# An SSM convolution with a gated feed-forward block, forward and backward: weight transposes through DRAM in pieces, stores on another queue, and gate tiles in rotating roles

## The chip, the core and the metric

The kernel runs on one core of a Trainium2 chip. A core has engines with queues of their own that work in parallel: TensorE (PE: matmuls; its weight loads are shown as PEld), VectorE (DVE), ScalarE (ACT), GpSimd (POOL) and SyncE (SP). SP, ACT and POOL also issue transfers (DMAs) between on-chip memory (SBUF) and DRAM; all of them are carried by the same 16 DMA engines. Matmul results go to PSUM, whose banks are shared out among the stages. Each queue is executed in order: an instruction that waits holds up everything behind it.

The metric is the time of one execution on the device in microseconds (us). Lower is better.

## What is computed

The reference is a forward pass and its vector-Jacobian product. With L = 2048, D = 576, F = 4608 and N = 128:

```python
x  = A_u                                   # [1, 2048, 576]
xn = layernorm(x)
# A: diagonal state-space model as a long convolution
K  = einsum("dn,dnl,dn->dl", C, exp(dt*A*l), dt*B).real
s  = irfft(rfft(xn, 2L) * rfft(K, 2L))[:L] + xn * Dskip
# B: gated feed-forward block
gate, up = xn @ w1, xn @ w3                # [2048, 4608] each
h  = silu(gate) * up
g  = silu(h @ w2)
out = x + s * g
# outputs: out, and the gradients of out against grad_out for
# x, A_re, A_im, B_re, B_im, C_re, C_im, log_dt, Dskip, w1, w3, w2
```

The backward part that matters here: the gradient arriving at the output of `h @ w2` is called go. From it come the gradient of h (`go @ w2.T`), from that the gate gradients GG (of gate) and GU (of up), the three weight gradients, and the input gradient `GG @ w1.T + GU @ w3.T` plus what comes back through the convolution.

## The kernel before

Rows of the sequence are cut into 16 tiles of 128 (LT), F into 36 blocks of 128 (FT) or 18 groups of 256 (NG, FG), D into four chunks of 128 and one of 64 (`cfg.dch`). The order of work in each queue is not written out by hand. Each piece of code sets a due time with `self.at(us)`, and the framework orders the instructions of every engine by due time and readiness. The due times are nominal: the profile runs later than they say.

The stages, with the times at which they run in the profile:

- **Prologue and SSM kernel, feed-forward hidden** (to about 525 us): layer norm, the convolution kernel K (written as Q, E and PZ parts to DRAM), and `ffn_hidden`, which stores gate and up to `GI_dram` and h to `H_dram`.
- **Forward tail** (`forward_tail`, 525 to about 800): per tile, h is read back transposed (hc) and multiplied with w2 (L873), then `g_all` (Silu) and `go_o` (its derivative) are taken from PSUM (L877), and the convolution runs in quarters. `last(m)` (L900) multiplies `go_o` with the convolution's result, transposes it on PE through one PSUM bank `ptr` (L907 to L913) into the four tiles `goT`, and writes `out_0` by tiles `x_t` of four row tiles.
- **Groups** (`backward`, 18 groups, about 790 to 1632). `phase6_load` loads a group's rows of w2, transposes them by DMA on SP (`w2T`, L1235), loads gate and up as `gg_n` and `h_n` from `GI_dram` on POOL's queue (L1239, L1240) and forms the activations. `phase6_group` computes `ph = go @ w2.T` (L1267), copies it to `gh` (three buffers), multiplies it into `gu_n` and `gg_n` (L1273), takes the w2 gradient in `phase6_grad2` (L1295), stores `GU_dram` and `GG_dram` in halves on SP's queue (L1280) and takes the w1 and w3 gradients in `phase6_grad13` (L1314 to L1322). The tiles gg_n, h_n and gu_n have two buffers each, so group gi + 2 uses those of group gi, in the same roles.
- **Convolution backward** (`ssm_bwd_conv`), in four quarters, runs on PE and VectorE between the first ten groups (to about 1310). It reads spectra (`a<-UH_dram`, `a<-KH_dram`) and `gs` on SP's queue and writes `GXN_dram` there (L1040).
- **Parameter gradients** (`param_quarter`, 36 chunks of 16 channels) follow from about 1290 to 1875. Each chunk transposes two halves of `Q_dram` by DMA on SP (`qT`, five buffers) and multiplies them on PE (L1065). About three chunks run beside each of the last eight groups, twelve beside the input stage. `phase5_final` closes them on VectorE and stores the gradients by `self.dma`, which alternates between SP and ACT (L80).
- **Input stage** (`phase6_inputs`, about 1650 to the end). For each row tile i, GG and GU are read back transposed by DMA on SP (`ggc`, `guc`, 36 blocks each, two buffers each), then PE adds 36 x 2 x 2 matmuls into `px` (L1357) against w1 and w3 transposed (`wT`). VectorE adds `GXN` (L1360), and `ln_bwd_tile` does the layer-norm backward and stores `out_1` through `self.dma`.

The transposed weights `wT` are made by DMA transposes on SP in `load_wT` (L1207): blocks 0 to 11 of w1 and w3 by ten instructions with due time `T2 - 150` (T2 is the nominal start of the input stage), blocks 12 to 35 by ten more inside the first tile of the input stage, into a pool `x_wB` that is opened after the groups' pools (among them the two buffers of gate tiles) and the go tiles (`gctx`) are closed.

All DMA transposes go through one helper, so in the profile they share line L1218 and are told apart by tile.

Of the kernel before, what the change touches and what calls it, by code (L numbers as in the profile page):

```python
# [11 lines left out]
ALU = mybir.AluOpType  # L12
# [47 lines left out]
class K:  # L60
# [759 lines left out]
    def forward_tail(self, T0, TB, TQ, gctx):  # L820
# [14 lines left out]
        gop = gctx.enter_context(pool(name="go_keep", bufs=1))  # L835
# [4 lines left out]
        with pool(name="g_all", bufs=1, side="right") as gp, pool(name="o_ep", bufs=3, side="right") as ep, \  # L840
# [9 lines left out]
            with pool(name="o_ep1", bufs=1) as ep1, pool(name="o_h", bufs=2) as hp, \  # L850
                    pool(name="o_w", bufs=1) as wpool, pool(name="o_ps", bufs=2, space=PS) as pso:
# [6 lines left out]
                for i0 in range(0, LT, 2):  # L858
# [10 lines left out]
                    for k, fs in runs:  # L869
# [5 lines left out]
                        if fs.stop == FT:  # L875
                            for o, fn in ((g_all, ACT.Silu), (go_o, ACT.Derivative_silu)):
                                nc.scalar.activation(out=o[:, i0 + k, :].rearrange("p (a b) -> p a b", a=2),  # L877
                                                     in_=pos[k][:, :, 0:D // 2], func=fn)
# [15 lines left out]
            gtp = gctx.enter_context(pool(name="go_t", bufs=1))  # L894
            self.goT += [gtp.tile([P, DT, KT * P], BF16, name=f"goT{m}") for m in range(NB // 2, NB)]
            for t_ in self.goT:
                nc.gpsimd.memset(t_[rem:P, nfull, :], 0.0)
            with pool(name="o_x", bufs=2, side="right") as xp:

                def last(m):  # L900
                    tsl = slice(m * KT, (m + 1) * KT)
                    for i in range(m * KT, (m + 1) * KT):
# [4 lines left out]
                        ptr = tps.tile([P, 1024], BF16, name="ptr")  # L907
# [7 lines left out]
                    x_t = xp.tile([P, KT, D], BF16, name="x_t")  # L915
                    nc.gpsimd.dma_start(out=x_t[:], in_=rows("A_u", m))
                    for i in range(m * KT, (m + 1) * KT):
                        s = self.perm(self.KT[:, i, :])
                        nc.vector.tensor_tensor(out=self.nat4(g_all[:, i, :]), in0=self.nat4(g_all[:, i, :]), in1=s,
                                                op=ALU.mult)  # L920
                    nc.vector.tensor_tensor(out=x_t[:], in0=g_all[:, tsl, :], in1=x_t[:], op=ALU.add)
                    nc.sync.dma_start(out=rows("out_0", m), in_=x_t[:])
# [35 lines left out]
    def conv_bwd_quarter(self, g, kp, zp, ps, T0, TQ):  # L958
# [68 lines left out]
        for j in range(NB):  # L1027
# [12 lines left out]
            nc.sync.dma_start(out=self.GXN_dram[:, j * KT:(j + 1) * KT, cs], in_=gx[:])  # L1040
# [36 lines left out]
    def phase5_final(self, out, big, S_all, ps2):  # L1077
# [6 lines left out]
        if True:  # L1084
# [3 lines left out]
            for c, (do, dsz) in enumerate(cfg.dch):  # L1088
# [20 lines left out]
                for src, oname in ((grho, "out_2"), (gth, "out_3")):  # L1109
                    ob = fo.tile([P, N], BF16, name="gout")  # L1110
                    nc.vector.tensor_scalar(out=ob[v], in0=src[v], scalar1=dtc, scalar2=None, op0=ALU.mult)
                    self.dma(aps[oname][do:do + dsz, :], ob[v])
# [20 lines left out]
                for (Xr, Xi, on_r, on_i) in ((self.B_re, self.B_im, "out_6", "out_7"), (self.C_re, self.C_im, "out_4", "out_5")):  # L1133
# [10 lines left out]
                    self.dma(aps[on_r][do:do + dsz, :], ob[v])  # L1144
                    ob2 = fo.tile([P, N], BF16, name="gout")
                    nc.vector.tensor_scalar(out=ob2[v], in0=gi_[v], scalar1=dtc, scalar2=-1.0, op0=ALU.mult, op1=ALU.mult)
                    self.dma(aps[on_i][do:do + dsz, :], ob2[v])
# [13 lines left out]
    def backward(self, T0, TG, TQ, TC, TX, gctx, mats):  # L1161
# [10 lines left out]
        with ExitStack() as out:  # L1172
            ffn = ExitStack()
            wp = ffn.enter_context(pool(name="e_w", bufs=2))
            elp = ffn.enter_context(pool(name="e_el", bufs=3))
            gwp = ffn.enter_context(pool(name="e_gw", bufs=2))
            rowp = ffn.enter_context(pool(name="e_w2r", bufs=1))
            inp = ffn.enter_context(pool(name="e_in", bufs=2))
# [6 lines left out]
            ps = out.enter_context(pool(name="b_ps", bufs=3, space=PS, side="right"))  # L1185
            self.ssm_bwd_conv(T0, TQ, ps)
# [4 lines left out]
            self.at(T2 - 150)  # L1191
            wT = [self.load_wT(wA, 0, FA)]
# [5 lines left out]
            for gi in range(NG):  # L1198
                nxt = self.phase6_load(gi + 1, T0 + TG * gi, TG, wp, inp) if gi + 1 < NG else None
                self.at(T0 + TG * gi)  # L1200
                self.phase6_group(gi, cur, elp, gwp, ps_h, ps_gw)
                cur = nxt
            ffn.close()
            gctx.close()
            self.phase6_inputs(T2, TX, FA, wT)

    def load_wT(self, pool, f0, f1):  # L1207
        cfg = self.cfg
        tiles = []
        for w in ("B_w1", "B_w3"):  # L1210
# [272 lines left out]
```

## Time and profile before

Three runs took 2050.96, 2056.60 and 2060.35 us. The profiled execution took 2050.93 us.

| quantity | value |
|---|---|
| median of the runs | 2056.6 us |
| profiled execution | 2050.93 us |
| its span | 2049.2 us |
| PE busy | 1753.0 us, 86% of the span |
| PEld busy | 1282.2 us |
| DVE busy | 1284.2 us |
| ACT busy | 940.1 us |
| POOL busy | 272.9 us |
| mean granted PE clock | 0.94 |
| moved by DMA | 448.92 MB, mean 219 GB/s |
| SP and ACT queue q1 | 615952 packets, 294.84 MB |
| POOL's queue q0 | 27952 packets, 126.24 MB |
| one weight transpose on SP (wTB_w) | 1.29 / 2.80 / 4.91 us (min, median, max), 20 of them |
| one half-chunk transpose on SP (qT) | 2.06 / 3.02 / 6.66 us, 72 of them |
| one gate-tile transpose on SP (guc) | 4.76 / 5.52 / 12.44 us, 16 of them |

How to read it: the profile is one execution. Busy time is the time in which an engine executes an instruction; for a queue marked SPq or POOLq the time is that of issuing a transfer, and what ends it can be a full queue. A row of the timeline has start, duration, engine, line, operation, destination and sources, the count, and in brackets the idle time of that engine just before and what released it. A row of the stretches has the busy time of each engine with the number of instructions, then PE's granted clock as a share of full speed, the mean share of time in which the 16 DMA engines were busy (it can exceed 1 slightly), and the bytes per second. A row of the waits has engine, line and what it waited for, then us in total, how often, and the longest.

### The profile page before, as it was taken

The page shows a single profiled execution, that of the slowest core. Times are in us where ns is not written, and L with a number is a line of the kernel's source. Part 1 is how long each engine was busy: PE and PEld are TensorE (multiplying, and loading weights), DVE is VectorE, ACT ScalarE, POOL GpSimd, SP SyncE. Part 2 cuts the span into 40 slices and gives each one's busy share as a digit, 9 for nine tenths or more (in the row PEclk, how much of TensorE's full clock was granted, in tenths as well). Part 3 has the DMA queues.
Part 4 walks back from the last instruction along what each step waited for, and adds up shares of the span by engine and source line. Part 5 has one row for each costly group of instructions (what it writes and reads, how often), then busy time and mean ns, then how long its engine had stood idle before and what let it go on. Part 6 is the DMA issues. An engine that isn't in the chain of part 4 may idle for free.

```text
span 2049.2 us, 39303 instructions
## 1 busy us (share of the span) xinstructions
PE 1753.0 (86%) x16050; PEld 1282.2 (63%) x16104; DVE 1284.2 (63%) x2646; ACT 940.1 (46%) x1512; POOL 272.9 (13%) x347
## 2 busy tenths in 40 slices
PE   3779999999699995999999999778888827889868
PEld 1444444444488874878878887667767715668656
DVE  9468888978287723596967979345565532446622
ACT  5658888988445544745445454344544200000000
POOL 4113333433312103000000000000000000000000
PEclk9889999999899997999999999888999958999989
DMA  4868999998956569375664646999999799999683
GB/s 130 282 270 296 369 372 376 358 362 327 302 139 174 137 140 262 112 211 174 186 190 135 200 129 204 236 224 227 219 216 228 176 206 214 230 197 186 124 159 85
DMA packets 681861, 448.92 MB, mean 219 GB/s; under 512 B 477136, under 2 KB 640848, under 8 KB 671952
## 3 DMA queue, kind: packets, MB, share of 16 engines
q1 hardware_dynamic: 615952, 294.84, 58.8%
q0 software_dynamic: 27952, 126.24, 17.3%
q10 hardware_dynamic: 37776, 25.32, 4.6%
q8 instruction: 126, 2.06, 0.4%
q14 instruction: 55, 0.45, 0.1%
HBM read 128.29 MB, written 206.88 MB: 164 GB/s over the span
## 4 chain that ended last, share of the span: by engine, by line
PE 34%; DVE 18%; DMA 11%; SPq 4%; ACT 3%; issue 2%; POOL 0%; ACTq 0%; DVEq 0%; POOLq 0%
PE px L1357 10%; PE pgw L1314 8%; SPq L1218 4%; PE po L873 4%; PE ph L1267 4%; DMA qT<-Q_dram 3%; PE pgw L1295 3%; DVE cm_t L696 3%; DMA guc<-GU_dram 3%; DVE cm_t L693 2%; DVE Z L694 1%; DMA gg_n<-GI_dram 1%; PE et_ps L715 1%; DVE Z L699 1%; DVE Z L698 1%
## 5 line engine op out<-in xcount | busy, mean ns | idle before, releaser
L1357 PE MATMUL px<-wTB_w,guc 128*128 128x288 bf16 x1152 | 245.9, 294 | 45.6 <-DMA guc<-GU_dram 32.1
L808 PE MATMUL pgu<-wmB_w,xnT 128*128 128x512 bf16 x1106 | 279.3, 381 | 4.0 <-ACT E L447 0.9
L1357 PE MATMUL px<-wTB_w,ggc 128*128 128x288 bf16 x1152 | 246.8, 295 | 32.4 <-DMA wTB_w<-in_B_w_dram 14.3
L1314 PEld LDWEIGHTS <-xn_bf 128*128 128x128 bf16 x2304 | 225.0, 98 | 34.0 <-issue 7.4
L1070 DVE TENSOR_TENSOR pr_q<-et_ps,pz 128x512 f32<-128x512 f32 x144 | 93.9, 682 | 190.9 <-PE et_ps L1065 112.8
L1267 PE MATMUL ph<-w2T,goT 128*128 128x256 bf16 x1440 | 194.4, 287 | 1.9 <-DMA w2T<-w2r 1.2
L808 PEld LDWEIGHTS <-xnT 128*128 128x128 bf16 x1152 | 102.9, 97 | 125.0 <-issue 24.7
L1374 ACT ACTIVATE t<-gx 128x576 f32<-128x576 f32 x16 | 10.9, 683 | 362.9 <-DVE gx L1360 346.3
L1357 PEld LDWEIGHTS <-guc 128*128 128x128 bf16 x1152 | 115.1, 100 | 85.7 <-DMA guc<-GU_dram 37.8
L1295 PE MATMUL pgw<-go_o,h_n 128*128 128x288 bf16 x1152 | 158.1, 292 | 7.6 <-DVE h_n L1249 7.6
L1267 PEld LDWEIGHTS <-goT 128*128 128x128 bf16 x1440 | 143.6, 103 | 28.5 <-issue 1.6
L1357 PEld LDWEIGHTS <-ggc 128*128 128x128 bf16 x1152 | 115.3, 101 | 59.1 <-issue 12.9
L873 PE MATMUL po<-w2g,hc 128*128 128x288 bf16 x1152 | 148.5, 286 | 3.0 <-DMA hc<-H_dram 3.0
L1316 ACT CAST gw<-pgw 128x256 bf16<-128x256 f32 x144 | 53.6, 372 | 195.6 <-PE pgw L1314 195.4
L1360 DVE TENSOR_TENSOR gx<-px,gxs 128x288 f32<-128x288 f32 x32 | 13.3, 451 | 204.2 <-PE px L1357 204.1
L1295 PEld LDWEIGHTS <-h_n 128*128 128x128 bf16 x1152 | 113.6, 100 | 37.4 <-DVE h_n L1249 8.1
L1314 PE MATMUL pgw<-gu_n,xn_bf 128*128 128x256 bf16 x1152 | 131.7, 272 | 5.0 <-ACT gw L1299 3.1
L873 PEld LDWEIGHTS <-hc 128*128 128x128 bf16 x1152 | 111.2, 98 | 30.6 <-DMA hc<-H_dram 3.7
L1314 PE MATMUL pgw<-gg_n,xn_bf 128*128 128x256 bf16 x1152 | 128.7, 273 | 0.0
L1270 ACT CAST gh<-ph 128x512 bf16<-128x512 f32 x144 | 80.5, 591 | 87.3 <-PE ph L1267 57.4
L813 ACT CAST gu_t<-pgu 128x1024 bf16<-128x1024 f32 x108 | 110.3, 1022 | 8.6 <-DMA GI_dram<-gu_t 8.4
L811 ACT ACTIVATE s_t<-pgu 128x512 bf16<-128x512 f32 x144 | 87.7, 610 | 39.3 <-PE pgu L810 38.4
(323 smaller groups left out, 3489.3 us busy)
## 6 DMA issues: line engine op xcount, KB each, us to landing
GI_dram<-gu_t POOLq DMA_DIRECT2D x72, 512.0 KB, 7.8
Q_dram<-q_k SPq DMA_DIRECT2D x36, 1024.0 KB, 7.5
E_dram<-E_k POOLq DMA_DIRECT2D x18, 1152.0 KB, 5.5
E_l<-E_dram SPq DMA_DIRECT2D x36, 576.0 KB, 8.9
H_dram<-h_t SPq DMA_DIRECT2D x72, 256.0 KB, 7.7
gg_n<-GI_dram POOLq DMA_DIRECT2D x18, 1024.0 KB, 5.9
h_n<-GI_dram POOLq DMA_DIRECT2D x18, 1024.0 KB, 8.2
GU_dram<-gu_n SPq DMA_DIRECT2D x36, 512.0 KB, 5.0
```

Of the source, the lines that this page charges most:

```text
L696: tt_(out=f(t2), in0=f(B)[:, :, ::-1], in1=Az.rearrange("p q k d -> p q (k d)")[:, :, None].to_broadcast([P, Q, 2, KT * Wq]), op=ALU.mult)
L808: nc.tensor.matmul(pgu[:, j], lhsT=xnT[:, c, ts], rhs=wm[w][:, c, :], start=(c == 0), stop=False)
L811: nc.scalar.activation(out=s_t[:, :, q, :], in_=pgu[:, 0].rearrange("p (g f) -> p g f", g=ng), func=ACT.Silu)
L813: cp(out=gu_t[:, :, :, q, :], in_=pgu[:].rearrange("p u (g f) -> p u g f", g=ng))
L873: nc.tensor.matmul(pos[k][:, pi_, 0:pw], lhsT=hcs[k][:, fi, :], rhs=w2[fi][:, po:po + pw], start=(fi == 0), stop=(fi == FT - 1))
L1070: nc.vector.tensor_tensor(out=pr[:, s].rearrange("p k r x -> p r k x"), in0=T[:], in1=pz[:, s:s + 2, h * 8:h * 8 + 8, :].rearrange("p r d ...
L1218: self.nc.sync.dma_start_transpose(out=dst, in_=src)
L1267: nc.tensor.matmul(ph[j][:, k, :].rearrange("p (a f) -> p a f", f=P), lhsT=lw, rhs=rh, start=(n == 0), stop=(n == nfull))
L1270: nc.scalar.copy(out=gh[:, j], in_=ph[j][:])
L1295: nc.tensor.matmul(pgw[pi_][:, 0:pw], lhsT=hn[:, tt, fl * P:(fl + 1) * P], rhs=go_o[:, tt, po:po + pw], start=(tt == 0), stop=(tt == LT - 1))
L1314: nc.tensor.matmul(pw_[:, 0:FG], lhsT=self.xn_bf[:, tt, c * P:(c + 1) * P], rhs=nat[:, tt, :], start=(tt == 0), stop=(tt == LT - 1))
L1357: nc.tensor.matmul(px[pi_][:, 0:pw], lhsT=act[:, fi, :], rhs=wT[part][ai][:, f, po:po + pw], start=(fi == 0 and ai == 0), stop=(fi == FT - ...
```

## The change

**Weights through DRAM.** A scratch tensor `WT_dram` [2, 128, 36, 576] is added. During the first ten groups, 40 pieces (w1 and w3 by turns, quarters of nine blocks, five channel chunks) are transposed on SP into one small tile `wTp` and stored to `WT_dram` from POOL's queue, a piece every quarter of a group. Later `wT` is loaded from there by plain transfers on POOL's queue: blocks 0 to 11 with due time `T2 - 100`; 12 to 21 in the last group into gate tiles of the last but one group; 22 to 29 into the go tiles `goT` at `T2 - 0.5 * TG`; 30 to 33 into `x_wB`, and 34 and 35 into what is left of a gate tile.

**Input stage.** The gate tiles are no longer in a pool of their own: even row tiles use the memory of `go_o`, odd ones that of the last group's gate tiles, in parts. For row tile 0, blocks 0 to 33 are transposed before the last group's stores, 34 and 35 after.

**Queues.** GU/GG stores, parameter-gradient stores and the `out_1` stores go from SP (or SP and ACT by turns) to POOL.

**Gate tiles.** One buffer each of six tiles a0, b0, z0, a1, b1, z1; the roles of a and b change every second group, so group gi + 2 has its gg where group gi had its h_n, and the other way round. The gg load is due 0.4 group earlier.

**Smaller parts.** `gh` has two buffers and not three; pools are opened in another order; the derivative is taken before Silu; a second PSUM bank serves every other go transpose of the last two `goT` tiles; `x_t` holds two row tiles; the memset of `goT` is due earlier; `GXN_dram` is written in two halves in the order in which the input stage reads it, and VectorE adds in place there.

```diff
@@ forward_tail
-                            for o, fn in ((g_all, ACT.Silu), (go_o, ACT.Derivative_silu)):
+                            for o, fn in ((go_o, ACT.Derivative_silu), (g_all, ACT.Silu)):
...
-                        ptr = tps.tile([P, 1024], BF16, name="ptr")
+                        ptr = (tps2 if m >= NB // 2 and i % 2 else tps).tile([P, 1024], BF16, name="ptr")
...
+                    for i0 in range(m * KT, (m + 1) * KT, HT):
+                        x_t = xp.tile([P, HT, D], BF16, name="x_t")
...
@@ conv_bwd_quarter
-            nc.sync.dma_start(out=self.GXN_dram[:, j * KT:(j + 1) * KT, cs], in_=gx[:])
+            for h in range(2):
+                nc.sync.dma_start(out=self.GXN_dram[:, j * KT:(j + 1) * KT, :].rearrange(
+                    "p t (h g d) -> p t h g d", h=2, g=4)[:, :, h, g], in_=gx[:, :, h * W // 2:(h + 1) * W // 2])
@@ phase5_final (and the three stores after it)
-                    self.dma(aps[oname][do:do + dsz, :], ob[v])
+                    nc.gpsimd.dma_start(out=aps[oname][do:do + dsz, :], in_=ob[v])
@@ backward
+            inp = gctx.enter_context(pool(name="e_in", bufs=1))
+            gwp = ffn.enter_context(pool(name="e_gw", bufs=2))
+            wtp = ffn.enter_context(pool(name="e_t", bufs=1))
+            elp = ffn.enter_context(pool(name="e_el", bufs=2))
             wp = ffn.enter_context(pool(name="e_w", bufs=2))
-            elp = ffn.enter_context(pool(name="e_el", bufs=3))
-            gwp = ffn.enter_context(pool(name="e_gw", bufs=2))
             rowp = ffn.enter_context(pool(name="e_w2r", bufs=1))
-            inp = ffn.enter_context(pool(name="e_in", bufs=2))
+            gw2p = ffn.enter_context(pool(name="e_gw2", bufs=2))
...
+            self.WT_dram = self.dram.tile([2, P, FT, D], BF16, name="WT_dram")
+            for k in range(8 * len(cfg.dch)):
+                self.at(T0 + TG * (0.2 + 0.25 * k))
+                self.prep_wT(wtp, k)
...
-            self.at(T2 - 150)
-            wT = [self.load_wT(wA, 0, FA)]
+            self.at(T2 - 100)
+            wT = [[None] * FT, [None] * FT]
+            self.load_wT(wA, 0, FA, wT)
...
+                if gi == NG - 1:
+                    self.at(T0 + TG * gi)
+                    self.late_wT(inp, FA, wT)
...
+    def gate_tiles(self, gi, inp):
+        p, k = gi % 2, gi // 2 % 2
+        return [inp.tile([P, self.cfg.LT, self.FG], BF16, name=f"{n}{p}") for n in ("abz", "baz")[k]]
+
+    def prep_wT(self, pool, k):
         cfg = self.cfg
+        n = 9
+        assert cfg.FT == 4 * n
+        ai, q, c = k % 2, k // 2 // len(cfg.dch), k // 2 % len(cfg.dch)
+        do, dsz = cfg.dch[c]
+        t = pool.tile([P, n, P], BF16, name="wTp")
+        v = t[:].rearrange("p f d -> p (f d)")[:, 0:n * dsz].rearrange("p (f d) -> p f d", d=dsz)
+        self.nat_transpose(v, self.aps[("B_w1", "B_w3")[ai]][do:do + dsz, q * n * P:(q + 1) * n * P])
+        self.nc.gpsimd.dma_start(out=self.WT_dram[ai, :, q * n:(q + 1) * n, do:do + dsz], in_=v)
+
+    def wT_into(self, dst, ai, f0, wT):
+        n = dst.shape[1]
+        self.nc.gpsimd.dma_start(out=dst, in_=self.WT_dram[ai, :, f0:f0 + n, :])
+        for f in range(n):
+            wT[ai][f0 + f] = dst[:, f, :]
...
@@ phase6_load
-        gg = inp.tile([P, LT, FG], BF16, name="gg_n")
-        hn = inp.tile([P, LT, FG], BF16, name="h_n")
-        gu = inp.tile([P, LT, FG], BF16, name="gu_n")
+        gg, hn, gu = self.gate_tiles(gi, inp)
+        self.at(T - 0.4 * TG)
         nc.gpsimd.dma_start(out=gg[:], in_=self.GI_dram[gi, :, 0])
+        self.at(T)
@@ phase6_group
-                nc.sync.dma_start(out=dst[ts, :, gi * FG:(gi + 1) * FG].rearrange("t p f -> p t f"), in_=t_[:, ts, :])
+                nc.gpsimd.dma_start(out=dst[ts, :, gi * FG:(gi + 1) * FG].rearrange("t p f -> p t f"), in_=t_[:, ts, :])
@@ phase6_inputs
+            self.at(T2 - 0.5 * TG)
+            n = DT * self.cfg.KT * P // D
+            gts = [self.rows((self.gop if m < 2 else self.gtp).tile([P, DT, self.cfg.KT * P], BF16, name=f"goT{m}"), n)
+                   for m in range(4)]
+            for ai in range(2):
+                for j in range(2):
+                    self.wT_into(gts[2 * ai + j], ai, self.fl + n * j, wT)
...
+            FN = FT - self.FG // P
+            for ai, src in enumerate((self.GG_dram, self.GU_dram)):
+                self.nat_transpose(even[:, ai, 0:FN], src[0, :, 0:FN * P])
+            self.load_wT(wB, fl, FB, wT)
...
+            self.at(T2 - 0.3 * TG)
+            for ai, src in enumerate((self.GG_dram, self.GU_dram)):
+                self.nat_transpose(even[:, ai, FN:FT], src[0, :, FN * P:FT * P])
...
@@ ln_bwd_tile
-        self.dma(out1[i * P:(i + 1) * P, :], o1[:])
+        nc.gpsimd.dma_start(out=out1[i * P:(i + 1) * P, :], in_=o1[:])
```

## The prediction

> **What bounds the kernel now.** I read the page first, then the stretches, then the queues inside the stretches where TensorE (PE) stops. Columns of the first two rows: 40 slices of 51 us, busy tenths.
>
> ```profile
> PE   3779999999699995999999999778888827889868
> DMA  4868999998956569375664646999999799999683
> ```
>
> PE is busy for 1753.0 us of 2049.2, so 296 us are idle. From slice 26 on the DMA row stands at 9 while PE falls to 7 or 8, and once to 2. The stretches say how much each place loses (PE, PEld, DVE, ACT, POOL busy; PE's clock; DMA share; GB/s):
>
> ```profile
> 775.00:825.00 50.00, 28.28 (x215) 21.18 (x215) 22.60 (x53) 27.97 (x46) 16.27 (x29) 0.73 1.00 283
> 825.00:1300.00 475.00, 448.83 (x4644) 384.13 (x4643) 374.19 (x776) 238.30 (x472) 20.93 (x39) 0.99 0.59 173
> 1300.00:1350.00 50.00, 24.96 (x279) 20.82 (x278) 9.77 (x13) 10.26 (x17) 1.62 (x3) 0.73 1.10 235
> 1350.00:1632.00 282.00, 248.56 (x2660) 211.62 (x2659) 151.70 (x218) 117.74 (x198) 8.53 (x16) 0.94 0.97 215
> 1632.00:1700.00 68.00, 18.32 (x222) 12.80 (x219) 23.87 (x30) 0.37 (x1) 0.00 (x0) 0.60 1.07 207
> 1700.00:1875.00 175.00, 151.60 (x1429) 119.19 (x1428) 70.44 (x120) 6.21 (x16) 0.00 (x0) 0.93 1.12 212
> 1933.00:1971.00 38.00, 21.79 (x148) 15.61 (x148) 11.49 (x26) 2.33 (x6) 0.00 (x0) 0.72 0.80 119
> ```
>
> Length minus PE: 21.7 us idle between the forward tail and the groups, 26.2 in the first ten groups, 25.0 at 1300, 33.4 in the last groups, 49.7 before the input stage, 23.4 in its first half, 16.2 at 1933. The first ten groups are the only late stretch with DMA room (0.59). The timeline names what PE waits for in the two largest short stretches:
>
> ```profile
> 1318.32 18.03 SPq L1218 DMA_TRANSPOSE wTB_w<-in_B_w_dram  x8
> 1342.87 0.40 PE L1065 MATMUL et_ps<-gk_l,qT 128*128 128x32 bf16 x8 [23.53 <-DMA qT<-Q_dram]
> 1660.25 35.78 SPq L1218 DMA_TRANSPOSE wTB_w<-in_B_w_dram  x10
> 1693.52 0.40 PE L1357 MATMUL px<-wTB_w,guc 128*128 128x288 bf16 x1 [11.20 <-DMA wTB_w<-in_B_w_dram]
> ```
>
> At 1318 PE is not waiting for the weights themselves: its in-order queue stands at a qT matmul whose transpose is behind eight weight transposes on SP. At 1660 it needs the weights. The chain and SP's waits show the third place:
>
> ```profile
> 1932.36 0.28 DVE gout L1146
> ...
> 1954.56 15.73 DMA guc<-GU_dram
> ```
> ```profile
> SPq L80 <- DVE gout L1146: 16.0, 1, 16.0
> ```
>
> SP stands for 16.0 us at a store of a parameter gradient that VectorE has not written; the transposes of the next gate tiles are behind it.
>
> **The change, part by part.** The sum is made on the profiled execution: 2050.93 us, with 1.7 us around its span. The median of the runs, 2056.6, is 5.7 above that, and I carry the 5.7 over unchanged.
>
> 1. Early weight transposes (12 of 36 blocks each, ten instructions) leave SP at 1282 and 1318. Eight took 18.03 us on SP; PE's wait was 23.53. Gain 18 (bounds 18 and 23.5).
> 2. The late ten took 35.78 us on SP (24 blocks each). They go, and the first pair of gate tiles is transposed before the last group ends, 34 of 36 blocks of it. Idle there is 49.7, of which the 35.8 is the sure part. The remaining 13.9 is four chunks of qT work, which stays, and the wait for the first ggc/guc, which shrinks. Gain 42 (36 and 49.7).
> 3. Parameter stores on POOL's queue, which is empty after 1632 (busy 0.00). What is queued behind a waiting store there is only out_1. Gain 15, the 15.73 wait; bounds 0 and 16.2, nothing if VectorE's end of the parameters, which waits for the same stores to land (gout has three buffers), now comes last.
> 4. The plain loads: 2 x 4608 x 576 x 2 B = 10.6 MB. Between 300 and 500 us, plain transfers ran at 364 GB/s with the engines full: 29 us. About 3.5 MB (12 blocks) are due 100 us before the nominal input stage, 2.9 MB (ten blocks) in the last group, 4.1 MB (14 blocks) around its end, beside a DMA share of 0.97. They are not all on the path: the stretch 1575 to 1592 shows a share of 0.54 and 17.00 us of PE in 17, and the first px tile needs 17 us to walk its 36 blocks. Cost 10 (0 and 29).
> 5. The 40 pieces in the first ten groups. A piece has 9 blocks; an early transpose with 12 took 18.03 / 8 = 2.25 us, so 1.7 us, 68 us of SP and DMA in all. Then 40 stores, 10.6 MB in rows of 256 B (128 B for the last 64 channels): 29 us at 364 GB/s; the trace has no such store, and its 512 B rows (GU_dram, 512 KB) land in 5.0 us, so I allow half speed, 58 us. DMA share goes from 0.59 to 0.59 + (68 + 58)/475 = 0.86. PE's waits in this stretch are almost all for VectorE (Z, gx, gk_st, ZZ), with 1.4 us for a DMA, so the cover is that neither PE nor VectorE stands on transfers now. The added wait: one buffer wTp, so each transpose on SP waits until the former piece's store on POOL has landed. Behind it on SP stand w2T, the spectra loads a<-UH_dram and a<-KH_dram, gs and the GXN stores; PE waits for w2T, VectorE for the spectra. Cost 8 (0, and 126 if none of it hides).
> 6. GU/GG stores move from SP to POOL. POOL's queue already stands at loads that wait for PE:
>
> ```profile
> POOL gg_n L1239 <- PE pgw L1322: 116.7, 7, 23.2
> ```
>
>    Now a store may wait for VectorE (on SP 51.8 us in all) with w2r, h_n and the next gg load behind it; a group has 42 to 48 us, and each POOL issue is 0.54, so 72 stores are 39 us of its time. SP gets back 4 us a group (at 1358 to 1362: 0.53 + 0.58 + 1.48 + 1.41), but after those stores it stands anyway until PE frees a qT buffer (nothing issued from 1366 to 1376). Gain 3 (a loss of 51.8, the wait in full; a gain of 33.4, all the idle time of the last groups).
> 7. Rotating roles: the next-but-one group's gg goes to the tile of h_n, free after the second-weight gradient and not after the two others (14.13 + 2 us later). gg loads of 5.9 us are 3.7% of the chain inside 825 to 1310, 18 us. Gain 5 (0 and 15), since VectorE holds most of that chain.
> 8. Forward tail: derivative first, two PSUM banks for half of the go transposes, halves of x_t, and the first gg no longer behind them: at 802.54 the first gg load was issued behind an out_0 store, 28 us after the last forward matmul. Each go transpose cycles in 1.76 us with one bank; eight at up to half saved are 7. Gain 10 of 21.7 (0 and 16; goT still follows the last derivative).
> 9. gh from three buffers to two: ScalarE's copy may wait for VectorE. Waits of that kind are 1.1 us early and 6.5 us late now. Cost 2 (0 and 7.6).
> 10. GXN stored in two halves (16 more SP issues at 0.37, 6 us beside waits of 42), the add in place and one fewer temporary on VectorE (busy 70 of 175 us in the input stage): nothing; if uncovered, 6.
>
> Sum: -18 - 42 - 15 + 10 + 8 - 3 - 5 - 10 + 2 = -73. 2050.9 - 73 = 1978; with 5.7 the median is **1984**.
>
> Two rules weigh on parts 5 and 6. POOL's issues measure 0.53 to 0.54 us even between 900 and 925, where VectorE is busy 25.00 of 25. The Trainium skill, "SBUF — State Buffer", "SBUF: two separate sides", says that DMA descriptors from GpSimd starve while VectorE holds the shared port in its two-port modes; its section "A bandwidth-pool intuition that's wrong" has 620 ns becoming 3100. By it the 112 stores of parts 5 and 6 would cost an estimated 278 us more of POOL time, and the sum would turn to a loss if a third of it were on the path; the rows show no such stretching. "DMA: Bandwidth & Descriptors", "Specifications", puts line rate at 512 B and more, with read-modify-write below; by it the 256 B stores are worse than plain ones, as I allowed without it.
>
> **The rivals.**
> A, the sum: 1984, own range 1960 to 2014. Chance 0.50.
> B, only shifted: from 1350 on transposes pace everything (share 0.97 to 1.12 at about 210 GB/s), so the loads come back at the full 29 and the pieces at 15. -18 - 36 + 29 + 15 - 10 - 5 = -25, 2032. For it: the share. Against it: plain loads run at 364 GB/s, weight transposes at 7.1 MB / 35.8 us = 198. Chance 0.18.
> C, PE-bound throughout: gains at their far ends, 23.5 + 49.7 + 16.2 + 16, and half of the 33.4 in the last groups: -122, 1934. Against it: qT stays. Chance 0.14.
> D, slower: the one-buffer chain of part 5. Each piece's store sits in POOL's queue behind a load waiting up to 23.2 us, and SP stands as long with w2T behind. SP itself issues for some 16 us of a 47-us group (868 to 890), so it can stand for about 30 unnoticed; past that each us delays w2T. Four pieces a group with two of them behind the full 23.2 make 46, and with the issues 62 of 47 us; I take 10 of the 15 as lost in each of ten groups: +100, against the 73, 2056.6 + 27 = 2084. It decides from 7.3 us a group. For it: POOL stands for about 40 of each 47 us today. Against it: two pieces a group can go while it is free. Chance 0.12.
> E, the loads land late or early enough to change nothing, with the tail's gain lost too: 2057. Chance 0.06.
>
> **How the numbers follow.** The time is A's. The low end 1940 leaves out half of C (0.07); the high end 2045 leaves out D and a little of E and B (0.13). A measurement of this kernel tells about 0.5% from no change, 2046 to 2067. Faster: A, C and most of B, 0.82; same: E and the edge of B, 0.06; slower: D, 0.12.
>
> **What would show it.** Right: no weight transposes after about 1300; no PE wait of 23 us at the first qT; px starting within 10 us of the last group; four px tiles at the end with no gap before them; the first ten groups as long as before, near 47 us each, with DMA share 0.8 to 0.9. Wrong on 5: SP waiting for WT_dram stores, PE waiting for w2T. Wrong on 4: px waiting for weight loads, or PE for qT in the last three groups. Wrong on 3: px waiting at the end behind parameter work. The prediction as a whole fails if the first ten groups lengthen by more than 50 us, or if px starts on time but its tiles still take 20 to 23 us each.

## The result, and the profile after

After: 2161.1 us, the median of four runs (2154.5 to 2164.4), against 2058.5 for the kernel before beside it (2051.0 to 2068.7). The ratio is 1.049, with a 95% interval of 1.0437 to 1.0545: about 103 us slower. Two numbers in brackets behind a time below are this interval of the ratio to the kernel before, run beside it. The forecast was 1984 us, faster; its range ended at 2045. The profiled execution of r2_throwaway, one of the experiments, fell into a slower state (2185.6 us, its other three 2149.6 to 2168.6), so it is left out of that run's median, and its trace is read for the pace of its transfers alone.

The rows of 40 slices of the page of the kernel after (54 us each, busy tenths):

```profile
PE   3789999999399986967777989969888767789968
DMA  4869999997956568577688575799999999999783
```

Slices are counted from 0. The new hole stands where the kernel before had none: from slice 17 to 21 PE is at 6 and 7, where the row of before has 9s. The 3 in slice 10 is the start of the forward's output projection. The stretches of the kernel after (PE, PEld, DVE, ACT, POOL busy; PE's clock; DMA share; GB/s):

```profile
860.00:1230.00 370.00, 288.27 (x2808) 242.19 (x2807) 219.09 (x466) 141.57 (x301) 69.27 (x80) 0.89 0.71 174
1230.00:1401.00 171.00, 155.62 (x1626) 134.66 (x1624) 147.13 (x301) 78.09 (x152) 24.10 (x33) 0.97 0.69 191
1401.00:1775.00 374.00, 301.44 (x3126) 252.32 (x3125) 173.35 (x249) 138.36 (x231) 45.07 (x63) 0.90 1.02 225
```

and one of the kernel before, for the second:

```profile
860.00:1230.00 370.00, 348.87 (x3647) 299.13 (x3645) 299.83 (x626) 178.22 (x367) 17.18 (x32) 1.00 0.57 171
```

In the same 370 us PE starts 2808 matmuls instead of 3647, and VectorE does 466 instructions instead of 626: both wait. The DMA engines are not full (0.71), and after 1230 PE is back at 91%. The chain of waits that ends with the window, by line, kernel after:

```profile
by line: DMA wTp<-in_B_w_dram 48.0%; DMA WT_dram<-wTp 38.5%; issue 7.3%; DMA GXN_dram<-gx 1.3%; PE et_ps L671 1.3%; SPq L1267 1.0%; DMA a<-UH_dram 0.8%; DVE gx L1043 0.3%; POOL WT_dram L1241 0.3%; SPq L1045 0.3%; DVE a L679 0.2%; DVE gx L10
```

86% of it is pieces: transpose lands, store lands, next transpose. The window was cut where the last piece stands, so this chain shows the pace of the pieces, not yet that PE waits for them. The timeline of SP's queue and then of POOL, kernel after (start, length, what; in brackets idle time and its releaser):

```profile
860.35 38.04 SPq L1267 DMA_TRANSPOSE wTp<-in_B_w_dram  x5
898.44 2.61 SPq L1267 DMA_TRANSPOSE w2T<-w2r  x2
901.10 0.77 SPq L998 DMA_DIRECT2D out_dram<-gds_sb  x1
904.87 26.54 SPq L1267 DMA_TRANSPOSE wTp<-in_B_w_dram  x4
```
```profile
875.72 1.01 POOL L1241 DMA_DIRECT2D WT_dram<-wTp  x1 [8.52 <-issue]
876.73 0.58 POOL L1289 DMA_DIRECT2D a<-GI_dram  x1
884.98 1.00 POOL L1241 DMA_DIRECT2D WT_dram<-wTp  x1 [7.67 <-DMA wTp<-in_B_w_dram]
893.58 1.01 POOL L1241 DMA_DIRECT2D WT_dram<-wTp  x1 [7.60 <-DMA wTp<-in_B_w_dram]
```

Five pieces hold SP for 38 us, four more for 26.5; POOL waits some 7 to 8 us for each. The 40 start from 860.3 to 1227.2, 9.4 us apart, and the scheduler has put them into about six groups instead of ten, five and four in a row. The sums of the waits, two of SP's and one of POOL's, kernel after:

```profile
SPq L1267 <- DMA WT_dram<-wTp: 164.5, 38, 6.4
...
SPq L1267 <- DMA wTp<-in_B_w_dram: 84.5, 34, 8.8
```
```profile
POOL WT_dram L1241 <- DMA wTp<-in_B_w_dram: 278.1, 38, 12.3
```

SP stands at landings of pieces for 249 of these 367 us. How this reaches PE is in the waits of VectorE and PE from 860 to 1230, first the kernel after, then before:

```profile
DVE a L679 <- DMA a<-UH_dram: 24.7, 3, 12.9
...
DVE gx L1037 <- DMA GXN_dram<-gx: 23.8, 4, 8.8
```
```profile
PE et_ps L671 <- DVE gx L1043: 28.7, 3, 21.0
```
```profile
DVE gx L1033 <- DMA GXN_dram<-gx: 10.8, 3, 5.3
DVE a L679 <- DMA a<-UH_dram: 4.8, 2, 2.9
```
```profile
PE et_ps L671 <- DVE gx L1039: 2.4, 2, 1.4
```

All of VectorE's waits for transfers in this window come to 79.7 us, against 18.6 in the kernel before.

Where the time went, by the starts of the last matmuls of each part (us; "forward" is the last of the output projection, "convolution" the last inverse transform of the convolution's backward, "groups" the last weight gradient, then to the end of the span):

| profiled execution | forward | to convolution | to groups | to the end | span |
|---|---|---|---|---|---|
| before | 774.1 | 506.9 | 351.0 | 417.2 | 2049.2 |
| after | 804.3 | 596.8 | 373.3 | 388.2 | 2162.6 |
| r1_nopieces | 792.6 | 520.5 | 390.0 | 415.0 | 2118.1 |
| r1_twobuffers | 797.2 | 574.2 | 374.9 | 389.4 | 2135.7 |
| r1_poolorder | 782.7 | 597.8 | 366.4 | 396.1 | 2143.0 |
| r3_spread | 796.6 | 562.3 | 404.5 | 383.4 | 2146.8 |
| r3_gusp | 792.2 | 583.4 | 368.1 | 384.6 | 2128.3 |
| r4_before_pieces | 771.2 | 617.4 | 343.9 | 407.5 | 2140.0 |
| r4_before_tail | 783.3 | 516.7 | 355.6 | 415.5 | 2071.1 |
| r2_before_out8 | 775.3 | 505.2 | 355.9 | 403.1 | 2039.5 |

After against before: +30, +90, +22, -29. Each row is one execution. Eight kernels have the forward of the kernel after unchanged, and their profiled executions end it between 792.2 and 804.3; so some 10 us of a difference in that column can be the execution's, and the +30 is at the top of that spread.

### The profile page after: what moved, and what is told of

Its sections match the earlier page's. It is cut to its first block, busy times and chain, and to the rows that moved or that the text cites. A ratio compares the mean times of both kernels' runs of the same rounds, so it can differ in the third digit from the quotient of the medians.

```text
span 2162.6 us, 39640 instructions
## 1 busy us (share of the span) xinstructions
PE 1787.6 (83%) x16104; PEld 1299.3 (60%) x16104; DVE 1291.9 (60%) x2650; ACT 938.8 (43%) x1512; POOL 415.3 (19%) x523
## 4 chain that ended last, share of the span: by engine, by line
DMA 28%; PE 21%; DVE 10%; issue 10%; SPq 3%; ACT 2%; POOL 1%; ACTq 0%; POOLq 0%; DVEq 0%
DMA wTp<-in_B_w_dram 8%; DMA WT_dram<-wTp 7%; PE pgw L1363 6%; PE px L1430 5%; DMA qT<-Q_dram 4%; PE po L873 4%; SPq L1267 3%; DMA hc<-H_dram 2%; DVE cm_t L696 1%; DMA GXN_dram<-gx 1%; PE ph L1316 1%; PE et_ps L671 1%; DMA pz<-PZ_dram 1%; PE pgw L1344 1%; DVE S_all L1079 1%
## 5 line engine op out<-in xcount | busy, mean ns | idle before, releaser
L1316 PEld LDWEIGHTS <-goT 128*128 128x128 bf16 x1440 | 147.2, 105 | 45.9 <-issue 19.1
L1430 PEld LDWEIGHTS <-go_o 128*128 128x128 bf16 x1152 | 116.5, 102 | 82.5 <-DMA go_o<-GU_dram 35.9
L1363 PE MATMUL pgw<-z,xn_bf 128*128 128x256 bf16 x1152 | 138.9, 281 | 28.4 <-ACT gw L1365 18.2
L1446 ACT ACTIVATE t<-gxs 128x576 f32<-128x576 f32 x16 | 11.0, 685 | 327.1 <-DVE gxs L1433 318.1
L1433 DVE TENSOR_TENSOR gxs<-px,gxs 128x288 f32<-128x288 f32 x32 | 13.3, 452 | 178.4 <-PE px L1430 162.6
L1430 PE MATMUL px<-wT,go_o 128*128 128x288 bf16 x512 | 79.0, 316 | 47.3 <-DMA go_o<-GU_dram 34.1
L817 POOL DMA_DIRECT2D GI_dram<-gu_t x72 | 68.4, 949 | 177.2 <-DVE gu_t L813 73.2
L1241 POOL DMA_DIRECT2D WT_dram<-wTp x40 | 40.4, 1011 | 294.5 <-DMA wTp<-in_B_w_dram 278.1
L1344 PE MATMUL pgw<-go_o,b 128*128 128x288 bf16 x640 | 88.4, 291 | 5.2 <-DVE b L1298 5.2
L1071 PE MATMUL et_ps<-gk_l,qT 128*128 128x32 bf16 x1152 | 39.4, 179 | 63.5 <-DMA qT<-Q_dram 63.5
L1079 DVE TENSOR_REDUCE S_all<-pr_q 128x32 f32<-128x1024 f32 x72 | 87.2, 1211 | 0.2
```

Of the source, the lines that this page charges most:

```text
L817: nc.gpsimd.dma_start(out=self.GI_dram[fb * ng:(fb + 1) * ng, :, :, i0:i0 + NT, :].rearrange("g p u t f -> p u g (t f)"), in_=gu_t[:].rear ...
L1079: nc.vector.tensor_reduce(out=S_all[:, :, d0:d0 + 8], in_=pr[:].rearrange("p s k r (d a) -> p (s k) d r a", a=AV), op=ALU.add, axis=AX.XY)
L1316: nc.tensor.matmul(ph[j][:, k, :].rearrange("p (a f) -> p a f", f=P), lhsT=lw, rhs=rh, start=(n == 0), stop=(n == nfull))
L1344: nc.tensor.matmul(pgw[pi_][:, 0:pw], lhsT=hn[:, tt, fl * P:(fl + 1) * P], rhs=go_o[:, tt, po:po + pw], start=(tt == 0), stop=(tt == LT - 1))
L1363: nc.tensor.matmul(pw_[:, 0:FG], lhsT=self.xn_bf[:, tt, c * P:(c + 1) * P], rhs=nat[:, tt, :], start=(tt == 0), stop=(tt == LT - 1))
L1430: nc.tensor.matmul(px[pi_][:, 0:pw], lhsT=act, rhs=wT[ai][fi][:, po:po + pw], start=(fi == 0 and ai == 0), stop=(fi == FT - 1 and ai == 1))
```

## The experiments

**The pieces.** Theory: one buffer ties SP to POOL's store, and everything behind on SP's in-order queue waits. Rivals: the transposes themselves, or their place.

r1_nopieces:
```
-            for k in range(8 * len(cfg.dch)): ... self.prep_wT(wtp, k)
-        self.nc.gpsimd.dma_start(out=dst, in_=self.WT_dram[ai, :, f0:f0 + n, :])
+        for (do, dsz) in self.cfg.dch:
+            self.nat_transpose(dst[:, :, do:do + dsz], ...w1 or w3...)
```


> Undone: the weights' way through DRAM. The 40 pieces are gone and each later load is a set of direct DMA transposes on SP into the same destination; all else as changed. Theory (one small buffer makes SP and POOL walk in step, 9.25 us a piece from 860 to 1230): the stretch from the last forward matmul to the last convolution-backward matmul, 596.5 us changed and 506.6 before, returns to 505 to 520, and the direct transposes take some 25 to 60 us of it back later: total 2100 to 2135. Rival (the stretch grew because of gate tiles in rotating roles, two gh buffers and stores on POOL): the stretch stays above 560 and the total is 2160 to 2200.


Measured 2117.2 us, ratio 1.033 (1.0286 to 1.0369). The convolution stretch is back at 520.5, so 76 of the 90 us are the pieces'. The last groups and the end now pay for direct transposes: 390 + 415 against 373 + 388, 43.5 us. The same 370 us of this kernel:

```profile
860.00:1230.00 370.00, 348.68 (x3613) 296.99 (x3610) 285.44 (x605) 183.19 (x386) 43.19 (x60) 0.99 0.58 167
```

PE is as busy as before, to 0.2 us, and VectorE's waits for transfers in this window are down to 9.9 us.

r1_twobuffers: `e_t` with two buffers, and two rows w2r instead of four to make the room.


> Two wTp tiles in place of one (the memory comes from two w2 row tiles in place of four); the same transfers and bytes. Theory (standing in step): a piece's transpose can run while the former one's store lands, so 40 pieces take 200 to 240 us and not 370, and the stretch from forward end to convolution end falls by 40 to 60: total 2100 to 2125. Rival (the 21 MB more of transfers themselves slow the first ten groups): the stretch falls by under 10, total 2150 to 2162.


Measured 2134.5 us (1.036 to 1.0457). The 40 pieces take 205 us instead of 367, but the stretch falls by only 22.6, below the 40 to 60 of the theory and above the rival's 10.

r2_throwaway: the 40 transposes without their stores, late weights as in r1_nopieces.


> Leaves out the 40 stores of the pieces on GpSimd's queue; the 40 transposes stay as they are and their result is not used; the late groups transpose w1 and w3 directly, as in r1_nopieces. If the lockstep (SyncE waits for the one buffer's store, GpSimd for the transpose, 9.25 us a piece) makes the loss, the stretch from the last forward matmul to the last convolution matmul falls from 597 us to 525-545 us and the time to 2120-2145 us. If the transposes themselves (their room on the DMA engines and on SyncE's queue) make it, the stretch stays at 575-600 us and the time at 2170-2195 us.


Measured 2159.8 us (1.0458 to 1.0591), 43 above r1_nopieces, between the two ranges and in neither. The tile wTp in it:

```profile
L1267 SPq DMA_TRANSPOSE wTp<-in_B_w_dram x40: 1200/1292/3940, 849.1 to 1021.0; - x40
```

A piece still follows every 4.4 us (172 us over 39 steps). For 91.9 us of it SP waits until the transpose before has landed in the one buffer, so the run leaves out the store but not the whole wait.

r3_spread: three pieces a group over 14 groups.
```
+        self.nc.vector.tensor_copy(out=v[0:1, 0, 0:1], in_=x)   # x: an element of this group's gate tile
         self.nat_transpose(v, ...)
...
+            if s < 3 and 3 * gi + s < 8 * len(self.cfg.dch):
+                self.prep_wT(self.wtp, 3 * gi + s, gu[0:1, s * 4, 0:1])
```


> The kernel after, with the 40 pieces tied to the groups: three a group over 14 groups, each behind a one-element copy on VectorE from the gate tile that the group has just finished (in after, 40 in about six groups), and the first plain load at group 15. If the loss is SyncE's queue being overfull (six pieces of 9.25 us are 55 us in a group of 44), three a group (28 us) leave room: the stretch from the last forward to the last convolution matmul falls from 597 to 530-550 us and the time to 2105-2130 us. If each piece costs its 1.9 us (77 us / 40) wherever it stands, 575-600 us and 2145-2165 us.


Measured 2146.6 us (1.0426 to 1.0522). The time lies in the rival's range, the stretch (562.3) in neither. The convolution stretch gives back 34.5 us and the groups take 31.2. But the run does not settle what a piece costs on SP, because the copy that ties a piece to its group has to wait for the buffer too, now on VectorE:

```profile
DVE wTp L1239 <- DMA WT_dram<-wTp: 159.5, 20, 38.5
```

VectorE's queue stands there 72.9 us in the convolution stretch and 86.6 in the groups. The wait for the one buffer was moved, in part, from SP to VectorE.

r4_before_pieces: the pieces and the plain loads put into the kernel before (with gh in two buffers, for room).


> The kernel before with only the pieces and the plain loads (parts 1, 2, 4 and 5 of the prediction, and part 9: gh with two buffers to make room for wTp); the loads stand where before transposes the weights, 12 blocks 150 us before the nominal input stage and 24 at its start. If the pieces cost what the forecast's mechanism D and the run without them say (77 us in the convolution stretch) and the late transposes' gain is about 40 us (parts 1 and 2 less part 4: 50), 2085-2100 us. If the pieces cost so much only beside the change's other edits on the same queues (stores on GpSimd, rotating tiles), 2010-2050 us.


Measured 2144.0 us (1.0422 to 1.0512), 98 slower than before: by its size nearly the whole loss, with five of the ten parts in it, the second of them without the early gate transposes. The time is above both ranges expected. The convolution stretch is 110 longer, groups and end together 16.8 shorter. Two windows of it, the pieces standing from 771 to 1179:

```profile
1000.00:1200.00 200.00, 146.55 (x1425) 124.47 (x1424) 104.77 (x219) 79.23 (x165) 27.03 (x32) 0.84 0.66 168
1200.00:1400.00 200.00, 185.16 (x1922) 158.83 (x1920) 173.74 (x355) 95.50 (x182) 9.67 (x18) 0.99 0.59 184
```

PE stops losing when the last piece has gone. Two of the waits from 825 to 1300:

```profile
ACT L1258 <- DMA gg_n<-GI_dram: 78.2, 6, 18.4
```
```profile
PE ph L1281 <- ACT gh L1284: 46.2, 6, 16.5
```

ScalarE stood 6.1 us for the gate loads in the kernel before, and PE 0.6 us for gh. The gate loads are on POOL's queue, behind stores of pieces that wait for their transposes, so here POOL's queue is paid as well as SP's. How much of the 110 us belongs to gh with two buffers was not measured.

**The forward tail.** r1_poolorder: the pools of the kernel after in the order of before (o_ep1, o_h, o_w).


> Undone: only the order in which the three forward-tail pools are opened (o_ep1, o_h, o_w as before). Theory: the w2 loads of the forward tail start again at about 515 and not 534, no longer meet the first hc transpose (26.5 us), and PE's first forward-tail matmul is at about 548 and not 573: total 25 to 30 less, 2131 to 2136. Rival (hc is late for another reason, its own H_dram stores): under 5 less, 2156 or more.


Measured 2147.1 us (1.0429 to 1.052), 14 less than after, between the two ranges expected. The forward ends 21.6 us earlier than in the kernel after, 9.5 to 15.6 earlier than in the other seven kernels with that forward. The w2g loads on POOL's timeline, before, after (with the first hc transpose on SP's) and this run:

```profile
514.79 0.77 POOL L856 DMA_DIRECT2D w2g<-in_B_w_dram  x1 [1.06 <-PE et_ps L577]
```
```profile
534.43 5.97 POOL L856 DMA_DIRECT2D w2g<-in_B_w_dram  x8 [1.84 <-PE pgu L810]
```
```profile
534.16 26.52 SPq L1267 DMA_TRANSPOSE hc<-H_dram  x1
```
```profile
513.29 0.78 POOL L856 DMA_DIRECT2D w2g<-in_B_w_dram  x1 [1.07 <-PE et_ps L577]
```

With the change's order the weights' memory comes free only with the last hidden matmul (the releaser is pgu), 20 us later, and the loads meet the first hc transpose, which takes 26.5 us there (at most 12.9 in the kernel before).

r4_before_tail: the change's forward tail in the kernel before, pools in the order of before.


> The kernel before with the change's forward tail (derivative first, second PSUM bank, x_t in halves), but its pools in the order of before: part 8 without the reordering. The prediction's part 8 says 10 us faster, about 2040 us. If the 10-20 us that the forward stretches of r2_three and r3_spread_order_out8 still lack are these edits', 2060-2070 us.


Measured 2070.5 us (1.0051 to 1.0174), 24 slower than before by the medians. r5_tail_whole_x: the same, with x_t whole again.


> r4_before_tail with x_t in whole tiles again (derivative first and the second PSUM bank stay). In r4_before_tail the third and fourth rounds of half tiles stand on GpSimd ahead of the first gate load, each behind an out_0 store, and that load was issued 38 us after the last forward matmul where before has 28. If the halves make that, the load is back at 26-30 us and the time 8-14 us under r4_before_tail: 2056-2063 us. If derivative first and the second bank make the 23 us, 2066-2074 us.


Measured 2054.9 us (1.0004 to 1.0066): by the medians some 15 of the 24 are the half tiles. The chain of r4_before_tail between them and the first gate load:

```profile
809.35 2.26 DMA out_dram<-x_t
...
813.01 3.85 DMA x_t<-in_A_u_dram
...
821.79 7.96 DMA gg_n<-GI_dram
```

and the gate load on POOL's timeline of r5_tail_whole_x:

```profile
809.53 0.53 POOL L1241 DMA_DIRECT2D gg_n<-GI_dram  x1
```

Eight halves in two buffers are four rounds; the later ones wait for an out_0 store to land, and the gate load stands behind them: 38.2 us after the last forward matmul (783.6), against 28.3 here and 28.1 before.

**The stores.** r1_out8rows: out_8 as rows after one transpose on PE.
```
-    nc.sync.dma_start(out=aps["out_8"][0:nfull * P].rearrange("(c p) -> p c", p=P), in_=gl_bf[:, 0:nfull])
...
+    nc.tensor.transpose(pt[0:DT, 0, :], glogdt[:], self.ident_f[:])
...
+    nc.vector.tensor_copy(out=gl_t[:], in_=pt[0:DT, 0, :])
+    nc.sync.dma_start(out=aps["out_8"][0:nfull * P].rearrange("(c p) -> c p", p=P), in_=gl_t[0:nfull, :])
...
```


> out_8 (the gradient of log_dt, 576 values) is turned on PE and stored as rows of 256 and 128 bytes; before it is stored as single values of 2 bytes. Theory: these stores hold up every transfer behind them for some 15 us (19.0 us to landing, 23 GB/s from 2040 to 2060) and are the cause of PE's pause of 18.5 us at 2050 to 2100; without them 12 to 18 less, 2143 to 2149. Rival (the pause comes from transposes issued late, behind waits for VectorE): no change, 2159 to 2163.


Measured 2145.3 us (1.0413 to 1.0544), 16 less than after by the medians, with one run of the four above the lowest of after. What it removed, on SP's timeline of the kernel after:

```profile
2043.25 0.39 SPq L1160 DMA_DIRECT2D out_dram<-gl_bf  x1
2043.69 0.55 SPq L1162 DMA_DIRECT2D out_dram<-gl_bf  x1
2044.33 19.18 SPq L1267 DMA_TRANSPOSE go_o<-GG_dram  x1
2063.60 14.30 SPq L1267 DMA_TRANSPOSE go_o<-GU_dram  x1
```

Two short issues, then a transpose of 19 us where one takes 4.5 us at 2028 (the go_o<-GU_dram behind it, 14.3).

r2_before_out8: the same in the kernel before.


> The kernel before with only the store of out_8 as rows, by one transpose on TensorE. If the two-byte elements of that store hold the queues at the start of the last stage (1932-1950 us, 18-46 GB/s), the time falls by 12-18 us to 2033-2039 us and beats both kernels. If the gap is that of the first transposes themselves, within 4 us of before.


Measured 2032.5 us against 2049.7, ratio 0.992 (0.9885 to 0.9951): faster than both kernels. In the kernel before, the store that SP stood at for 16.0 us was late because VectorE itself waited for a parameter store to land, beside the out_8 stores:

```profile
1948.30 0.28 DVE L1143 TENSOR_SCALAR gout<-gr,dt_col 64x128 bf16<-64x128 f32 x1 [12.55 <-DMA out_dram<-gout]
```

In r2_before_out8 all of VectorE's waits of this kind are 5.3 us together, and SP's waits at parameter stores are at most 3.3 us each. r3_before_out8_pool: with the parameter stores on POOL as well, part 3.


> r2_before_out8 with the stores of the state-space parameters' gradients on GpSimd's queue, the change's third part alone. If SyncE's 16 us wait for VectorE at such a store held the gate transposes, as the prediction's part 3 has it, the time falls by 5-15 us to 2018-2028 us; if out_8 was all of that gap, the same as r2_before_out8 (2032.5) within 4 us.


Measured 2049.2 us (0.9953 to 1.0005): 17 slower than r2_before_out8 by the medians, the intervals just apart. SP's waits in its last stage:

```profile
SPq L80 <- DVE acc L1123: 14.3, 1, 14.3
SPq L1157 <- DVE gl_t L1156: 13.2, 1, 13.2
```

SP waits no less: two stores that stayed on it are reached earlier and wait for a later result of VectorE, 27.5 us where before had 16.0. r4_after_paramsp: part 3 undone in the kernel after.


> The kernel after with the stores of the parameter gradients back on SyncE's queue (part 3 undone). r3_before_out8_pool was 17 us slower with them on GpSimd's queue: if that holds here, 2144 us or less. If the wait is only handed on to out_8's stores, the same as after (2161) within 6 us. By the prediction's part 3, 2176 us.


Measured 2152.5 us (2140.1 to 2159.5; ratio 1.0452 to 1.0561): 9 under after, with overlapping runs. So part 3 is no gain in the kernel after either; that it costs time there is not shown.

r3_gusp: the GU and GG stores of the kernel after back on SP.


> The kernel after with the stores of GU and GG back on SyncE's queue, as before. If what r2_three_gusp showed (16 us less than r2_three) holds here too, 2145 us; if SyncE's queue, full of pieces, has no room for them in the first groups, 2155-2170 us.


Measured 2140.1 us (1.0387 to 1.047), 21 less than after. r5_before_gu_pool: part 6 alone on the kernel before.


> The kernel before with only the stores of GU and GG on GpSimd's queue (part 6 alone). By r3_gusp and r2_three_gusp (21 and 16 us), about 18 us slower than before: 2062-2072 us. By the prediction's part 6, 3 us faster: 2040-2050 us.


Measured 2057.3 us, ratio 1.0045 (1.0008 to 1.0082), some 10 slower than before, below the range expected. POOL's waits in it:

```profile
POOL GU_dram L1280 <- DVE gu_n L1273: 329.1, 30, 26.6
```

**Together.** r2_three: no pieces, pools as before, out_8 as rows.


> r1_nopieces, r1_poolorder and r1_out8rows together. If the three are separate terms they add: 2161 - 44 - 14 - 16 = 2087 us, with the first output-projection matmul near 550 us, and the rest above before (2051) is in the last groups, where w1 and w3 are transposed, 390 against 351 us. If they overlap (a later start hidden by a wait that stays), 2100-2117 us.


r3_spread_order_out8: the last two with r3_spread.


> r3_spread with the pools in the order of before and out_8 stored as rows. If the terms add, 30 us under r3_spread; if the forward's end stays late whatever the order (r2_three: forward end 793 us), 10-20 us under it.


r2_three_gusp and r4_five_undone add the GU/GG stores and then the parameter stores on SP.


> r2_three with the stores of GU and GG back on SyncE's queue. If those stores cost what I put on them in the prediction (moved at a gain of 3 us), this is the same as r2_three within 5 us. If on GpSimd's queue they hold back the loads of the gate tiles behind them (GpSimd waited 188 us in r1_nopieces' groups for the tile it is to store), the group stretch falls by 10-30 us and the time with it.

> r2_three_gusp with the parameter stores back on SyncE's queue as well: pieces gone, pools as before, out_8 as rows, and the GU, GG and parameter stores on SyncE. What it lacks to r2_before_out8 (2032.5) is the rest of the change: roles, gh, halves, the forward tail. If the parameter stores are worth 17 us here too, 2078 us; if not, 2090-2100 us.


Measured 2110.8 (1.0231 to 1.0335), 2130.9 (1.0361 to 1.0452), 2094.9 (1.0154 to 1.0285) and 2087.8 (1.0147 to 1.0249). The terms do not add: r2_three is 6 below r1_nopieces where 30 were open, and r3_spread_order_out8 is 16 below r3_spread. (In its profiled execution the forward of r2_three ends at 792.8, no earlier than in r1_nopieces; the other three, with the same forward, end it at 782.6 to 783.1.) The GU and GG stores on SP give 16 us again, the parameter stores 7 more, with overlapping runs. With five undone 55 us are left to r2_before_out8. Some 24 of it may be the forward tail; the roles, gh, the halves of GXN, the out_1 stores and the direct transposes at the late places are among the rest, and were not tried alone.

## Why the prediction was wrong

On the profiled executions the sum missed by 186 us, and the table says where. For the convolution stretch it had -7 (parts 5, 7 and 8), and +90 was measured, a miss of 97. For groups and end it had -68 (parts 1, 2, 3, 4 and 6), and -7 was measured, a miss of 61. For the forward it had no term, and +30 was measured.

The step that failed first is part 5: "Cost 8". The text named the wait, one buffer between SP and POOL, but gave its price no working: SP's time was taken as 40 x 1.7 us, the rate of transposes queued back to back. With one buffer a piece costs its latency: the transpose lands (median 4.0 us from its issue), POOL issues for 1.0, the store lands (3.7), and a piece follows every 9.4 us, 367 us of SP. In the kernel after, 76 of the 90 us are the pieces'; in the kernel before, together with gh in two buffers, they bring +110. Both lie inside the far end that the text kept, 126. The cover named there ("neither PE nor VectorE stands on transfers now") was not so even in the trace before: from 825 to 1300 VectorE stood 19.1 us for transfers (GXN 11.3, UH 5.4, gs 2.4). With SP's queue late the same transfers stop it longer, and PE waits for VectorE. The DMA share from 825 to 1300, forecast at 0.86, was 0.74: room on the DMA engines is no room on a queue.

Rival D named the mechanism and priced it at 100. Its sum, 2084, failed by taking the gains in full. Its detail was off, too: POOL's wait for PE was to hold the store, and mostly it was the transpose's own landing (278.1 us over the run). Against r1_nopieces, r2_throwaway with 172 us of pieces on SP loses 43 us of the time, r1_twobuffers with 205 loses 54 in the convolution stretch, and the kernel after with 367 loses 76. So the store's landing is a part, and the larger part stays without it. In both runs SP still waits for landings (91.9 us, and 105.9 by the same rows), so what the transposes would cost with no such wait is open.

- Parts 1, 2 and 4 (-50 together): 16.8 gained by the plain loads without the early gate transposes (r4_before_pieces). The late gap between the last weight gradient and the first px matmul did close, 21.5 us to 1.0 in the kernel after, and in the 88 us from there PE is busy 61.7 us instead of 32.7, though it still waits 14.4 us for gate tiles and 11.0 for qT. But the loads and the early gate transposes went into a stretch at a DMA share of 1.02, and a transpose beside them took 27 us:

```profile
1742.23 27.26 SPq L1267 DMA_TRANSPOSE go_o<-GG_dram  x1
```

- Part 3 (-15): no gain in either kernel. The last releaser was read as the cause: VectorE was late because a store before it was (12.55 us), and with out_8 as rows this goes; the change left out_8's two-byte elements in place. The 15.73 us taken as the gain were the landing of the transpose behind, not the wait.
- Part 6 (-3): some +10 alone, +21 in the kernel after, inside its far end of 51.8. The wait was handed to POOL and grew: it stands 329.1 us for gu_n where SP had stood 51.8, with gate loads and w2r behind. Its issues of these stores take 0.89 to 1.00 us in the kernel after, not 0.54.
- Part 8 (-10): some +24 without the reordering of pools, +14 by the reordering in the kernel after. "The first gg no longer behind them" was wrong: it stood behind twice as many. The memory order of pools was not costed at all.
- Parts 7, 9, 10: not tried alone. The chain of the kernel after has 17.23 us of GXN_dram<-gx at 1402, where part 10 had nothing.
- B's ground, transposes that pace everything from the last groups on, fits the share of 1.02 and the 16.8; its sum missed part 5 as A's did. C had nothing for it.
- The signs that the text set for itself held: SP waiting for WT_dram stores, and the first ten groups longer by more than 50 us.

## What to carry over

Cost a transfer through a single buffer as its whole latency, issue to landing twice, on every queue that takes part, and multiply by the count before looking at shares of DMA. A store moved off a waiting queue hands the wait to what stands behind it on the new queue and lets the old queue run into its next wait; follow both. The order in which pools are opened decides whose end frees the memory of a load: read it as a dependency.

## What the runs showed of the hardware

- 576 elements of two bytes, stored in two short issues, cost some 17 us. While they go, 20 us at a DMA share of 1.02 move 49 GB/s in the kernel after (2044 to 2064), and 18 us at a share of 0.35 move 20 GB/s in the kernel before (1932 to 1950). As rows the time falls by 17 us in the kernel before, and by 16 in the kernel after, there with overlapping runs.
- Where PE stood more, its granted clock was lower: 0.89 at 78% busy and 0.84 at 73% with the pieces (the kernel after and r4_before_pieces), 1.00 at 94% and 0.99 at 93% without (before, and r4_before_pieces after 1200). Matmuls of one form take longer in the window from 860 to 1230: the 457 of ph<-w2T,goT 291 ns where before has 275, the 128 of et_ps<-Z,dC 270 where before has 226. These two alone are 457 x 0.016 + 128 x 0.044 = 13 us.
- POOL issued the 40 stores with rows of 256 and 128 B in 0.99 to 1.08 us each, twice the 0.53 to 0.58 of its gate loads; the GU and GG stores took 0.89 to 1.00. The Trainium skill, "SBUF — State Buffer", "A bandwidth-pool intuition that's wrong", has a DMA from GpSimd's queue go from about 620 to 3100 ns beside a VectorE copy, because its descriptors wait for the shared port. The longest of these 40 issues is 1.08 us; whether VectorE held that port beside them no run here shows.
